# A fused recurrent-attention and cosine-gated MLP kernel: moving loads between queues and chunks

## The chip, the cores and the metric

The kernel runs on one core of a Trainium2 chip. The core has a matrix engine (TensorE, "PE" in the profile, with weight loads as "PEld"), three elementwise engines (VectorE or "DVE", ScalarE or "ACT", GpSimd or "POOL") and SyncE ("SP"), which in this kernel only issues transfers. Transfers can be issued from SP, ACT and GpSimd; in the profile the issuing is shown as SPq, ACTq and POOLq, and the transfer itself as DMA. The metric is the device time in microseconds of one launch.

## The reference

A linear recurrence over 768 steps for 4 x 8 heads of 40 channels, then a two-layer MLP whose activation is h cos(h).

```python
for t in range(S):
    y[:, :, t] = np.einsum('bhd,bhde->bhe', rt, state)
    Sa = np.einsum('bhde,bhe->bhd', state, at)
    state_decay = state * wt[:, :, None, :] - np.einsum('bhd,bhe->bhde', Sa, bt)
    state = state_decay + np.einsum('bhd,bhe->bhde', vt, kt)
...
h = x @ w_in          # x: the y of all heads, 3072 x 320; w_in: 320 x 2048
g = h * np.cos(h)
return g @ w_out      # 2048 x 320
```

The six inputs r, k, v, w (the decay), a and b have the form (4, 8, 768, 40) in float32; the two weight matrices are float64, and the kernel decodes the 64-bit words into float32 itself.

## The kernel before

**Tiling.** The sequence is cut into 24 chunks of 32 steps (C = 32, NCH = 24). In a chunk the recurrence becomes matrix products and the inverse of a triangular 32 x 32 matrix for each head. Four chunks share one inversion (a "quarter" q below is such a group of four chunks; there are six). The stages of a chunk are: p1 (w, a and b transposed, the matrix to be inverted), p2 (v, r and k, and the gram matrices), and main (t, q, x, s, z: the state transposed, read, solved and updated). The MLP is cut into pieces (first_a, first_b, second) that are put between the segments of the recurrence to keep TensorE filled.

**Order.** Everything is written out by hand: each engine runs its own instructions in program order. The function `step(work)` runs one segment and then counts down a list of postponed actions; `later(n, action)` puts an action at the end of the n-th step after it. Most transfers are issued in this way, so that n decides where in SP's queue they stand. A transfer that has to wait (for a buffer to be read, for data to be written) holds up all that SP has behind it.

**Inputs.** `load(c, names)` (lines 146 to 152) issues, for each named input of chunk c, four transfers of 40 KB, one for each batch. w, a and b have two buffers each in turn (nat_w0, nat_w1 and so on); chunks 2 and 3 use free space in the weight buffers w_in_sb and w_out_sb instead. So in the profile "w_out_sb<-in_b_dram" is b of chunks 2 and 3. For the first four chunks w is loaded as it is and its running products are made by a scan. From chunk 4 on the decays come already multiplied up: `ws_fetch(q)` (line 159) loads the decays of a quarter, 640 KB, into the single buffer ws; `ws_scan(q)` (line 166) multiplies them up on DVE; `ws_store(q)` (line 178) writes ws to a buffer wd in DRAM; and load reads w of chunks 4 and on from wd (the tile "wd" has two buffers). `scanned(q)` (line 906) calls the scan and postpones the store and the next fetch. Quarter 1 is scanned in the startup (line 996), quarter 2 in chunk 3 (line 1064).

**Weights.** `rounded` (line 224) decodes a block of 512 columns in four parts: fetch (the 64-bit words, line 237, up to 512 KB), taken (DVE splits off mantissa and exponent, lines 245 and 246; ACT makes exponent and sign), mantissa (DVE line 255, ACT line 258) and product (DVE line 261, GpSimd line 264). There are 20 blocks. Their parts are strung on a list, `w_steps`, in which product n is followed by the fetch of block n + 3 (from block 7 on), the mantissa of n + 1 and the taking of n + 2. From block 10 on the words rotate through three buffers (nt, u, inv), so the buffer of block n + 3 is free once the mantissa step of block n has read its words. The list is worked off a few parts at a time, in the startup and in chunks 1 to 3.

**Around the change.** The startup issues its loads in lines 182 to 201; GpSimd fills constants up to line 218. The loop over chunks begins at line 1049; for chunk 2 the segments are

```python
segs, fill = [t, F2, v, q, S2, k, M, x, M, F3, g, M, s, S3, M, z, M, M], (0, 2)
```

where M is an MLP piece. The MLP's input goes through DRAM: `tokens` (line 771) writes a chunk's output to xd (line 775) and `back` (lines 785 and 787) reads it as xT. TensorE's calls named busy, spare and "po<-idle" are filler matmuls on zeros.

Of the kernel before, what the change touches and what calls it, by code (L numbers as in the profile page):

```python
# [20 lines left out]
def kernel(  # L21
# [43 lines left out]
    nc = tc.nc  # L65
# [54 lines left out]
    for n, fill in (("w", 1.0), ("a", 0.0), ("b", 0.0)):  # L120
        for i in range(4):
            x = slice((i - 2) * H * DP, (i - 1) * H * DP)
            if i < 2:
                t = const.tile([P, H, DP], F32, tag=f"nat_{n}{i}", name=f"nat_{n}{i}")
            else:
                t = {
                    "w": w_in_sb[:, 0, late:], "a": w_in_sb[:, 1, late:], "b": late_out
                }[n][:, x].rearrange("p (h d) -> p h d", h=H)
# [4 lines left out]
    for n in "kvr":  # L133
        t = const.tile([P, H, D], F32, tag=f"nat_{n}", name=f"nat_{n}")
# [11 lines left out]
    def load(c, names, via=nc.sync, parts=range(B)):  # L146
        for n in names:
            for i in parts:
                at_c = src[n][i, :, c * C : (c + 1) * C, :]
                if n == "w" and c >= 4:  # L150
                    at_c = wd[c // 4][i, :, c % 4]
                via.dma_start(nat[n, c][blk[i], :, :D], at_c.rearrange("h t d -> t h d"))  # L152
# [3 lines left out]
    ws = const.tile([P, C, D], F32, tag="ws", name="ws")  # L156
    wd = {}

    def ws_fetch(q, via=nc.sync):
        n = 4 * C * D  # L160
        via.dma_start(
            ws.rearrange("p t d -> p (t d)"),
            bass.AP(w.tensor, w.offset + q * n, [[S * D, B * H], [C * D, 4], [1, C * D]]),
        )

    def ws_scan(q):
        n = 1
        while n < C:
            to = ws[:, 2 * n - 1 :: 2 * n]
            nc.vector.tensor_tensor(to, to, ws[:, n - 1 :: 2 * n], ALU.mult)  # L170
            n *= 2
        n = C // 4
        while n:
            to = ws[:, 3 * n - 1 :: 2 * n]
            nc.vector.tensor_tensor(to, to, ws[:, 2 * n - 1 : C - 1 : 2 * n], ALU.mult)
            n //= 2

    def ws_store(q):
        wd[q] = dram.tile([B, H, 4, C, D], F32, tag="wd", name="wd")
        nc.sync.dma_start(wd[q].rearrange("b h c t d -> (b h c) (t d)"), ws.rearrange("p t d -> p (t d)"))  # L180

    for c in range(2):
        load(c, "w", parts=range(2))
# [2 lines left out]
    load(1, "a", nc.scalar)  # L186
    for n, c in (("w", 2), ("w", 3), ("a", 2), ("a", 3), ("b", 2)):
        load(c, n)
    ws_fetch(1)
    load(3, "b")  # L190


# [24 lines left out]
    idle = const.tile([P, P], BF16, tag="idle", name="idle")  # L217
    nc.gpsimd.memset(idle, 0.0)
    tick = const.tile([P, 1], BF16, tag="tick", name="tick")

    WID = 512
    first_done, second_done = [], []
# [120 lines left out]
    def later(steps, work):  # L343
        waiting.append([steps, work])

    def step(work, of_inv=0, of_w=0, small=False):


        before = list(waiting)
        work()  # L350
        G["small"] = small and G["kind"]
        for w in before:
            w[0] -= 1
            if w[0] == 0:
                waiting.remove(w)
                w[1]()
        for steps, n in ((inv_steps, of_inv), (w_steps, of_w)):
            for _ in range(min(n, len(steps))):
                steps.pop(0)()
# [224 lines left out]
    def p2_in(c):  # L584
        for dst, m in ((vp, "v"), (rp, "r")):
            nc.gpsimd.tensor_copy(  # L586
                dst.rearrange("p (i f) d -> p f i d", f=2)[:, :, :, :D],
                nat[m, c].rearrange("p (f i) d -> p f i d", f=2),
            )
        landed(c)  # L590
# [312 lines left out]

        return [first_w, both_a, lambda: p1_b(c), lambda: p1_n(c)]

    def scanned(q):

        ws_scan(q)
        later(2, lambda: ws_store(q))
        if q + 1 < NCH // 4:  # L910
            later(12, lambda: ws_fetch(q + 1))

    def p2(c):
        def last():
# [14 lines left out]
    with tc.manual_schedule():  # L929
# [63 lines left out]
        w_work[1][0]()  # L993
        for seg in (other[1], *first[2:], *other[2:]):
            step(seg)
        scanned(1)
        p2_in(0)
        p2_kn(0)
        inv_space()
# [25 lines left out]
        busy(6)  # L1025
        step(z0, 0, 2)
        busy(4)
        for n, c, name in ((1, 4, "a"), (3, 4, "w"), (5, 5, "w"), (6, 5, "a"), (7, 5, "b"), (9, 4, "b")):
            later(n, lambda c=c, name=name: load(c, name))

        done = 0

# [8 lines left out]
        def allowed(c):  # L1041
            return done < len(pieces) and 2 * pieces[done][0] + 2 <= c
# [6 lines left out]
        for c in range(NCH):  # L1049
            t, q, x, s, z = main(c)  # L1050
            v, k, g = p2(c + 1) if c + 1 < NCH else [lambda: None] * 3
            q0 = c - c % 4 + 4
            fill, pn, pn4 = (1, 4), None, None
            if c == 0:
                segs = []
            elif c == 1:
                segs, fill = [t, F1, v, q, k, S1, x, g, s, z], (1, 4)
            elif c == 2:
                segs, fill = [t, F2, v, q, S2, k, M, x, M, F3, g, M, s, S3, M, z, M, M], (0, 2)
            elif c == 3:  # L1060
                pw4, pa4, pb4, pn4 = p1(4)
                pw, pa, pb, pn = p1(6)
                segs = [
                    t, pw4, M, q, pa4, M, x, lambda: scanned(2), M, s, pw, M, pb4, pa, M, pn4, M, z, M,
                    pb, v, pn, k, M, g,
                ]
                fill = (2, 3)
            elif c == 4:
                pw, pa, *p8 = p1(8)
                firsts = [lambda n=n: pair_first(4, n) for n in range(4)]  # L1070
                seconds = [lambda n=n: pair_second(4, n) for n in range(4)]
                F4, F5, F6, F7 = firsts
                S4, S5, S6, S7 = seconds
                segs = [
                    t, v, M, q, M, k, x, M, F4, M, S4, F5, M, s, F6, M, pw, F7, M, z, M, g, M, pa, S5, lambda: scanned(3),
                ]
                fill = (2, 0)
            elif c == 5:
                pw, pa = p1(10)[:2]
                pb, pn = p8  # L1080
                segs = [t, M, pb, q, M, pn, k, M, x, M, s, S6, M, z, M, S7, M, pw, v, M, g, pa, M]
            elif c % 4 == 0 and q0 < NCH:
                pb, pn = p1(q0)[2:]
                segs = [t, v, M, q, M, k, x, M, g, M, s, pb, M, z, M, pn, M, M]
                if q0 + 4 < NCH:
                    segs.insert(-1, lambda: scanned(c // 4 + 2))
            elif c % 4 == 1 and q0 < NCH:
                pw, pa = p1(q0 + 2)[:2]
                segs = [t, M, pw, q, M, x, k, M, s, v, M, z, M, pa, M, g, M, M]
            elif c % 4 == 2 and q0 < NCH:  # L1090
                pb, pn = p1(q0 + 2)[2:]
                segs = [t, M, pb, q, M, pn, v, M, x, M, s, k, M, g, M, z, M, M]
            elif c % 4 == 3 and q0 + 4 < NCH:
                pw, pa = p1(q0 + 4)[:2]
                segs = [t, M, pw, q, M, x, k, M, s, v, M, z, M, pa, M, g, M, M]
            else:
                segs = [t, v, M, q, M, x, k, M, g, M, s, M, M, z, M, M]
            n = len(segs)

            goal = 8 * (c + 1) - (18 if c < 19 else 20)  # L1100
            empty, places = 0, segs.count(M)
            if c > 3:
                empty = max(0, min(places - (goal - done), 2 if c < 8 else places))
                goal = max(goal, done + places - empty)
            place = 0
            if c == 19:
                shifted(N_PAD[c])
            for i, seg in enumerate(segs):
                kept_busy(FILL.get((c, i), 0))
                while seg is s and ("rt", c) not in G:  # L1110
                    if allowed(c):
                        piece(4, 0)
                    else:
                        inv_steps.pop(0)()
                while seg is pn4 and w_steps:
                    w_steps.pop(0)()
                if seg is not M:
                    G["kind"] = "q" if seg is q and c > 3 else "other"
                    step(seg, *((0, 0) if c < 3 and seg in (*firsts, *seconds) else fill), small=seg in (q, x, g, s, z, pn, pn4, *firsts, *seconds))
                    if seg not in (*firsts, *seconds) and (c < 2 or c == 2 and not done):  # L1120
                        busy({s: 6, q: 5, v: 4, k: 4, z: 4}.get(seg, 3))
                else:
                    place += 1
                    if place * empty // places > (place - 1) * empty // places:
                        continue
                    if allowed(c) and (c != 4 or done < 23):
                        piece(*fill)
                while i == n - 1 and c > 3 and done < goal and c != 4 and allowed(c):
                    piece(*fill)
                if seg is pn and (c == 3 or c > 4 and c % 4 == 2):  # L1130
                    inv_steps.extend(by_blocks(q0) if c == 3 else inverse(q0))
# [36 lines left out]
```

## Time and profile before

| what | value |
|---|---|
| median of 3 runs | 806.88 us (803.46 to 807.32) |
| the profiled execution | 806.77 us, of which the span of the profile is 805.0 us |
| PE busy | 752.7 us, 94% |
| DVE busy | 487.0 us, 60% |
| ACT busy | 387.8 us, 48% |
| POOL busy | 201.1 us, 25% |
| DMA | 55.78 MB, mean 69 GB/s |
| busy share of PE in 20 us slices, first to seventh, in tenths | 5 7 7 7 6 9 8, then 9 (the highest digit) but for the last |
| granted clock of TensorE | mean 0.973 |

Times in the views are microseconds from the span's start, with the duration behind them. In the chain of waits ("the chain of work that ended last") each line is what the work after it waited for; "issue" is time for which the profile shows no cause. In the timelines, a bracket at the end of a line gives the idle time of the engine before it and what ended it. In the table by stretches each row gives the stretch, its length, the busy time and the number of instructions of PE, PEld, DVE, ACT and POOL, the granted clock, the DMA share and GB/s.

### The profile page before, as it was taken

The numbers are of one execution on the slowest core, as the hardware profiler recorded it, in microseconds if no ns is written. First come the engines' busy times: TensorE is split into PE (matmuls) and PEld (weight loads), VectorE is DVE, ScalarE is ACT, GpSimd is POOL, SyncE is SP. The second block draws the span as 40 slices with busy tenths as digits, with TensorE's granted clock in tenths as the row PEclk, the third lists the DMA queues.
The fourth block names the chain that finished last, engine by engine and source line by source line (L and its number), as shares of the span: only waits on it lengthen the run. The fifth ranks groups of instructions, "written<-read, shape, count | busy, mean of one in ns | idle before, by whom it ended". The sixth has DMA issues, their size and how long they took to land.

```text
span 805.0 us, 39600 instructions
## 1 busy us (share of the span) xinstructions
PE 752.7 (94%) x17812; PEld 575.5 (71%) x17812; DVE 487.0 (60%) x1025; ACT 387.8 (48%) x723; POOL 201.1 (25%) x354
## 2 busy tenths in 40 slices
PE   5777698999999999999999999999999999999997
PEld 4544376777777777777777777777787777777775
DVE  8779658864734796553895644994346873333231
ACT  1337467555425435545435635535645445354352
POOL 5316535320322220330330230332131122201000
PEclk9688799999999999999999999999999999999999
DMA  8666552354253324334214314223220222101000
GB/s 114 176 162 149 143 145 74 57 121 65 59 125 58 66 38 71 72 92 67 60 40 69 94 36 72 53 45 69 46 46 21 46 46 49 24 17 34 19 17 16
DMA packets 183303, 55.78 MB, mean 69 GB/s; under 512 B 157152, under 2 KB 178656, under 8 KB 183136
## 3 DMA queue, kind: packets, MB, share of 16 engines
q1 hardware_dynamic: 177440, 52.11, 30.1%
q8 instruction: 140, 2.29, 1.2%
q10 hardware_dynamic: 5440, 0.82, 0.7%
q0 software_dynamic: 256, 0.33, 0.2%
q14 instruction: 27, 0.22, 0.1%
HBM read 42.07 MB, written 11.14 MB: 66 GB/s over the span
## 4 chain that ended last, share of the span: by engine, by line
PE 66%; DVE 18%; ACT 4%; issue 4%; DMA 3%; SPq 3%; POOL 1%; DVEq 0%; ACTq 0%; POOLq 0%
PE ph L101 23%; PE po L101 19%; PE x0ps L101 3%; PE dps L101 3%; SPq L152 3%; DVE inv_tmp L494 3%; DVE rw L395 3%; PE vT L330 3%; PE gram L101 2%; DVE inv L498 2%; PE sps L101 2%; PE nps L101 2%; PE qps L101 2%; PE sT L654 1%; DMA nat_a<-in_a_dram 1%
## 5 line engine op out<-in xcount | busy, mean ns | idle before, releaser
L101 PE MATMUL po<-w_out_sb,gT 128*128 128x320 f32 x768 | 223.1, 439 | 0.0
L101 PE MATMUL ph<-xT,w_in_sb 128*128 128x256 f32 x768 | 187.0, 388 | 0.3 <-issue 0.3
L101 PEld LDWEIGHTS po<-w_out_sb,gT 128*128 128x128 f32 x768 | 140.2, 190 | 54.2 <-issue 1.7
L101 PEld LDWEIGHTS ph<-xT,w_in_sb 128*128 128x128 f32 x768 | 140.1, 191 | 30.4 <-issue 12.5
L829 ACT ACTIVATE turns<-ph,rnd 128x512 f32<-128x512 f32 x96 | 64.1, 686 | 157.7 <-PE ph L101 157.3
L831 DVE SCALAR_TENSOR_TENSOR turns<-turns,ph 128x512 f32<-128x512 f32 x96 | 64.1, 685 | 111.7 <-ACT turns L829 111.4
L839 DVE TENSOR_TENSOR gT<-ph,turns 128x512 f32<-128x512 f32 x96 | 65.8, 687 | 39.1 <-ACT turns L836 39.1
L755 POOL TENSOR_TENSOR qz<-qz,wc 128x160 f32<-128x160 f32 x92 | 42.4, 480 | 167.1 <-DVE qz L754 166.5
L836 ACT ACTIVATE turns<-turns,half_pi 128x512 f32<-128x512 f32 x96 | 69.4, 723 | 3.1
L835 ACT ACTIVATE turns<-turns 128x512 f32<-128x512 f32 x96 | 60.2, 627 | 18.9 <-DVE turns L831 18.9
L101 PE MATMUL ph<-xT,w_in_tail 64*128 64x256 f32 (+1 forms) x512 | 54.9, 393 | 1.3 <-issue 1.3
L498 DVE TENSOR_TENSOR inv<-inv,inv_tmp 128x31 f32<-128x31 f32 (+15 forms) x124 | 51.2, 413 | 4.3
L754 DVE TENSOR_TENSOR qz<-dps,qz 128x160 f32<-128x160 f32 x92 | 29.2, 318 | 36.2 <-PE dps L101 36.0
L586 POOL COPY vp<-nat_v 128x320 f32<-128x320 f32 x24 | 11.9, 494 | 156.3 <-DMA nat_v<-in_v_dram 135.8
L494 DVE TENSOR_TENSOR inv_tmp<-u,inv 128x31 f32<-128x31 f32 (+15 forms) x124 | 48.6, 392 | 2.3
L395 DVE RECIPROCAL rw<-nat_w 128x320 f32<-128x320 f32 x20 | 42.9, 2144 | 0.1
L658 ACT COPY s<-sT 128x512 f32<-128x512 f32 x46 | 24.5, 585 | 35.1 <-PE sT L654 35.1
L101 PEld LDWEIGHTS ph<-xT,w_in_tail 64*128 64x128 f32 (+1 forms) x512 | 32.5, 160 | 10.4 <-issue 6.8
L766 POOL TENSOR_TENSOR yt<-yt,wb 128x512 f32<-128x512 f32 x24 | 31.9, 1329 | 22.3 <-DVE yt L761 22.3
L718 DVE TENSOR_TENSOR sm<-sps,su 128x128 f32<-128x128 f32 x48 | 11.7, 286 | 32.1 <-ACT sm L713 29.3
L396 POOL TENSOR_TENSOR bn<-nat_b,rw 128x320 f32<-128x320 f32 x22 | 20.1, 914 | 43.6 <-DVE rw L395 37.2
L642 ACT COPY vvm<-gram 128x256 f32<-128x256 f32 x24 | 8.8, 369 | 43.6 <-DVE ag L637 43.2
(136 smaller groups left out, 1127.9 us busy)
## 6 DMA issues: line engine op xcount, KB each, us to landing
words<-in_moe_w_in_dram SPq DMA_DIRECT2D x8, 512.0 KB
xd<-yt SPq DMA_DIRECT2D x48, 80.0 KB
out_dram<-ot SPq DMA_DIRECT2D x24, 160.0 KB
nat_k<-in_k_dram SPq DMA_DIRECT2D x92, 40.0 KB
nat_v<-in_v_dram SPq DMA_DIRECT2D x92, 40.0 KB
nat_r<-in_r_dram SPq DMA_DIRECT2D x92, 40.0 KB
nat_a<-in_a_dram SPq DMA_DIRECT2D x84, 40.0 KB
ws<-in_w_dram SPq DMA_DIRECT2D x5, 640.0 KB
```

Of the source, the lines that this page charges most:

```text
L101: nc.tensor.matmul(o, lhsT=lhsT, rhs=rhs, start=start, stop=stop, skip_group_check=True)
L395: nc.vector.reciprocal(rw, wn)
L494: nc.vector.tensor_tensor(tmp, u[:, j : j + 1, :j].to_broadcast([P, C - j, j]), x[:, j:, j : j + 1].to_broadcast([P, C - j, j]), ALU.mult,)
L498: nc.vector.tensor_tensor(x[:, j:, :j], x[:, j:, :j], tmp, ALU.subtract)
L754: nc.vector.tensor_tensor(z, pick(dp, 0, (2 * N72 + C, 2), (N72, 2), (1, D)), z, ALU.add)
L755: nc.gpsimd.tensor_tensor(z, z, wc.rearrange("p (f m b) -> p f m b", f=2, m=2)[:, :, :, bb] .unsqueeze(3).to_broadcast([P, 2, 2, D]), ALU. ...
L766: nc.gpsimd.tensor_tensor(yt.rearrange("p j b t -> p (j b) t"), yt.rearrange("p j b t -> p (j b) t"), wx, ALU.mult)
L829: nc.scalar.activation(n, u, ACTF.Identity, bias=rnd, scale=1.0)
L831: nc.vector.scalar_tensor_tensor(n, n, -ROUND, u, ALU.add, ALU.subtract)
L835: nc.scalar.activation(n, n, ACTF.Abs)
L836: nc.scalar.activation(n, n, ACTF.Sin, bias=half_pi, scale=-2.0 * math.pi)
L839: nc.vector.tensor_tensor(gT[:, 2 * e : 2 * e + 2].rearrange("p f t -> p (f t)"), us[e], ns[e], ALU.mult)
```

## The change

The fetch of decays for quarters 1 and 2 and the store of quarter 1 are issued by GpSimd instead of SP. The fetch for quarter 1 moves from between b of chunk 2 and b of chunk 3, on SP, to behind GpSimd's last constant; b of chunk 3 thus follows b of chunk 2 directly. The store of quarter 1 is postponed by 12 steps instead of 2, and the fetch of quarter 2 by 26 instead of 12. The loads of a, b and w for chunks 4 and 5 are registered at the start of chunk 2 instead of the end of the startup, with other numbers of steps and in another order. Quarter 2's store and the later fetches and stores stay on SP with their steps.

```diff
-    def ws_fetch(q, via=nc.sync):
+    def ws_fetch(q):
         n = 4 * C * D
-        via.dma_start(
+        (nc.gpsimd if q < 3 else nc.sync).dma_start(
             ws.rearrange("p t d -> p (t d)"),
...
     def ws_store(q):
         wd[q] = dram.tile([B, H, 4, C, D], F32, tag="wd", name="wd")
-        nc.sync.dma_start(wd[q].rearrange("b h c t d -> (b h c) (t d)"), ws.rearrange("p t d -> p (t d)"))
+        (nc.gpsimd if q == 1 else nc.sync).dma_start(wd[q].rearrange("b h c t d -> (b h c) (t d)"), ws.rearrange("p t d -> p (t d)"))
...
         load(c, n)
-    ws_fetch(1)
     load(3, "b")
...
     tick = const.tile([P, 1], BF16, tag="tick", name="tick")
+    ws_fetch(1)
...
-    def scanned(q):
+    def scanned(q, store=2, fetch=12):
 
         ws_scan(q)
-        later(2, lambda: ws_store(q))
+        later(store, lambda: ws_store(q))
         if q + 1 < NCH // 4:
-            later(12, lambda: ws_fetch(q + 1))
+            later(fetch, lambda: ws_fetch(q + 1))
...
-        scanned(1)
+        scanned(1, 12, 26)
...
-        for n, c, name in ((1, 4, "a"), (3, 4, "w"), (5, 5, "w"), (6, 5, "a"), (7, 5, "b"), (9, 4, "b")):
-            later(n, lambda c=c, name=name: load(c, name))
...
             elif c == 2:
+                for n, m, name in ((2, 4, "w"), (3, 4, "a"), (5, 5, "w"), (7, 5, "a"), (9, 4, "b"), (11, 5, "b")):
+                    later(n, lambda m=m, name=name: load(m, name))
```

## Prediction

> **What bounds the kernel now.** I read the page, then the chain of waits in order of time, then the timelines of SP, DVE, GpSimd and TensorE for the first 170 us, then the DMA busy share by tens of microseconds. From about 133 us TensorE is busy 92 to 100% of every stretch and its filler matmuls are fixed instructions, so what is won or lost earlier shifts everything behind it by the same amount. The change moves transfers only (the program's TensorE and DVE instructions stay the same 2621 and 932 rows in both listings), so it can pay only where somebody waits for a transfer, before 133 us. Two such places carry the argument. First the chain at the start, then the same chain around 90 us:
>
> ```profile
> 21.32 3.65 DMA w_out_sb<-in_b_dram
> 25.13 0.96 POOL bn L396
> 26.14 1.13 PE bT L330 x4
> 30.93 1.04 ACT nt L459 x2
> 31.99 1.26 DVE u L486
> ...
> 86.40 5.80 DMA words<-in_moe_w_in_dram
> ...
> 93.06 0.61 DVE w_out_sb L261
> ...
> 93.74 0.63 POOL w_out_sb L264
> ...
> 96.35 1.89 PE sT L654 x6
> ```
>
> At the start, the last piece of b of chunk 3 (it lands in w_out_sb) needs 3.65 us and releases GpSimd's product, the transposes, and DVE's u. At 86.40 a word block of w_in takes 5.80 us and releases the decoding of weights. What SP did before that issue, and what DVE and TensorE did meanwhile:
>
> ```profile
> 18.99 0.68 SPq L161 DMA_DIRECT2D ws<-in_w_dram  x1
> ...
> 79.06 3.28 SPq L152 DMA_DIRECT2D nat_a<-in_a_dram  x4
> 82.38 1.93 SPq L152 DMA_DIRECT2D nat_r<-in_r_dram  x4
> 84.41 1.89 SPq L152 DMA_DIRECT2D nat_b<-in_b_dram  x4
> 86.40 0.39 SPq L237 DMA_DIRECT2D words<-in_moe_w_in_dram  x1
> ```
> ```profile
> 78.35 0.68 DVE L255 SCALAR_TENSOR_TENSOR mant<-words,mant 128x512 f32<-128x512 uint32 x1
> ...
> 86.20 0.87 DVE L255 SCALAR_TENSOR_TENSOR mant<-words,mant 128x512 f32<-128x512 uint32 x1
> 92.30 0.43 DVE L245 TENSOR_SCALAR mant<-words 128x512 int32<-128x512 int32 x1 [5.22 <-DMA words<-in_moe_w_in_dram]
> ```
> ```profile
> 92.48 0.38 PE L101 MATMUL busy<-idle 128*128 128x512 bf16 x1 [3.64 <-issue]
> ...
> 95.37 0.69 PE L654 MATMUL sT<-ident,qz 128*128 128x128 f32 x2 [2.02 <-DVE yt L761]
> ```
>
> The block fetched at 86.40 is the eleventh (number 10); its buffer (nt) was freed by the mantissa step of block 7, at 78.35 + 0.68 = 79.03. SP was not waiting for a buffer but issuing loads of chunks 3 to 5 without a pause from 73.8 to 86.3. DVE stood still for 5.22 us, and its additions to the state (L754), queued behind, with it.
>
> **What the Trainium skill says.** "Runtime: NRT & Kernel Launch", Instruction fetch mechanics: instructions come in blocks of 16 KiB, 256 instructions, over a DMA queue of the sequencer, mostly hidden. The trace agrees on the block (the instruction queue q8: 140 packets, 2.29 MB, 16.4 KB each) but not on hidden: TensorE's "issue" waits inside runs of equal matmuls are 0.9 to 2.1 us at 50.8, 56.9, 64.0, 72.4 and 76.4, and 3.64 at 88.8, each ending 2.2 to 3 us after such a packet. "DMA: Bandwidth & Descriptors", Queues, rings and completion order: each DMA engine takes turns between queues by packet. So an instruction block stands behind data in flight; the longest wait falls where two word blocks and eight nat loads are in flight. "SBUF — State Buffer", SBUF: two separate sides: descriptors of a DMA issued from GpSimd are written by GpSimd, and some DVE operations lock it out. The trace of before has only eight such issues, 4.78 us in all, 0.60 each, and no such clash.
>
> **The change part by part.**
>
> *Fetch of ws for quarter 1, from SP to GpSimd.* SP loses 0.68 us ahead of b of chunk 3, and 640 KB that filled the 16 engines from about 20.9 to 23 (74 and then 100% busy, by the DMA view). b of chunk 2, with nothing such in front, landed some 1.7 us after its last issue; b of chunk 3 took 3.65. With the last issue at 20.6 it lands near 22.5 instead of 24.97. Then what is late next: the reciprocal at L395 ends at 23.02, and TensorE reaches this transpose at 24.5 (bT of chunk 2 begins at 23.85). The transpose moves from 26.14 to 24.5, DVE's u from 31.99 to about 30.4; the ws scan ends at 29.28 and is no obstacle. Gross gain 1.6. Against it: the 640 KB now run around 11.5 to 13.5 us, where the engines are 77% busy with chunks 1 to 3, and 1.7 us of them must go between. The slack there is 0.5 us for w (ACT's copies end at 15.3, DVE takes them at 15.9) and 1.3 for a (wn ends at 19.6, its reciprocal starts at 20.87). I take a loss of 0.4, net 1.2, ends 0.2 and 1.9. On GpSimd the issue stands before copies that are needed at 12.66 (aT): 1.8 us of slack against 0.6 for an issue.
>
> *Store of quarter 1, from SP at 34.73 to GpSimd behind rp of 62.81.* Behind it stand kn (L593), the copy at L594 and weight products; kn ends at 64.73 and its transpose starts at 68.23, so 0.6 us is hidden, even 2 us would be. On SP 1.34 us leave a stretch that DVE's inversion bounds: 0. Its transfer now lies beside DVE-bound work (58 to 87 us): 0.
>
> *Fetch of quarter 2, from SP at 55.16 to GpSimd behind the product of 102.99.* It frees 1.55 us of SP and 640 KB around the TensorE waits at 50.8 and 56.9: 0.2, ends 0 and 1.3. GpSimd is idle 2.5 us after its new place. The scan that needs it starts at 149.60: 46 us of cover.
>
> *The six loads of chunks 4 and 5 (24 issues of 0.47 us, 11.3 us of SP at least) leave 56 to 88 us.* Behind block 9, SP keeps only v and r of chunk 3 (8 x 0.48, done by 77.6), so block 10 is issued at 79.1 and lands by 85 even at 5.80 us. DVE needs it at 86.20 + 0.87 = 87.07 instead of 92.30: 5.2 us. Late next: GpSimd's state products would start at 89.7 instead of 94.86, so sT could run at 91.2; but TensorE has its own wait at 88.84. The block it waits for is asked for about 87.0; in the new order blocks 11 and 12 are in flight then, without nat loads. I take 1.8 of the 3.64 us, so TensorE is back at 90.6, has 1.0 of filler, and runs sT at 91.7: gain 4.6. Ends: 3.0 (the wait stays) and 5.2.
>
> *The same loads in chunk 2.* In the listing for SP, w and a of chunk 4 now stand between the store of xd and the return xT, which feeds the first ph matmuls. Eight issues are 3.8 us; SP idled 1.6 of them at 99.9 to 101.5 waiting for xd. So xT is issued 2.2 us later against the rest; it was issued by 103.0, lands about 2 us later, and is needed at 106.94, so 1.9 of cover: 0.3, ends 0 and 1.5 (the ws fetch meets it). Blocks 14 to 17 stand behind further loads. By SP's sum they land at 106.6, 115.5, 119.5 and 122, against needs (shifted by 4.6) of 106.7, 114.8, 118.4 and 125.9. DVE then waits 0.7 and 1.1, in front of idle gaps of 1.16 and 1.12 us: 0.2, up to 1.5. Last, TensorE's instruction blocks. Here it is never idle between 97 and 123, with packets of q8 every 4 to 5.5 us; DMA is 44 and 67% busy:
>
> ```profile
> 100.00:110.00 10.00, 10.00 (x315) 7.50 (x310) 5.67 (x9) 7.23 (x13) 5.44 (x5) 0.99 0.44 111
> 110.00:120.00 10.00, 10.00 (x296) 8.40 (x287) 6.14 (x13) 6.47 (x12) 1.42 (x2) 1.00 0.67 186
> ```
>
> The last number but one is the DMA share. A nat load of 40 KB costs some 3.4 us of one engine (141 to 161 us: 30% of 16 engines for 28 loads), so 24 of them and the ws fetch add about 110 of the 16 x 25 us: 80% or more. [...] I take 0.8 us over the five blocks, ends 0 and 5 x 1.5 = 7.5. Loss of the part: 0.3 + 0.2 + 0.8 = 1.3.
>
> *Sum.* -1.2 - 0.2 - 4.6 + 1.3 = -4.7 us. The profiled execution took 806.77 (span 805.0 and 1.8 around it), the median is 806.88, 0.1 above: 802.
>
> **The rivals.** (A) *The gap closes only to TensorE's own wait, and chunk 2 asks for more.* For it: 3.64 us of "issue" lie in the same gap. Against: most waits of that kind are under 2.1. Start -0.8, gap -3.0, chunk 2 +1.9: 805. (B) *All of it pays.* For it: DVE and ACT have idle gaps of 1 to 3 us all through chunk 2, and the waits at 50.8 to 57.8 shrink too. -1.9 - 1.0 - 5.2 + 0.3 = -7.8: 799. (C) *Slower: instruction blocks in chunk 2.* One mechanism: loads put into the one stretch in which TensorE has no slack delay its instruction fetches, five by 1.5 us (7.5) and the one in dps by 3.6, as at 88.84, 11 in all, against 6.0 won before: 812. It decides as soon as these waits exceed 6 us. For it: the DMA share; against: no such wait in 106 to 120, with word blocks at 74 to 82% in pieces of it. (D) *The loads of chunks 4 and 5 come late for chunk 3*: w is transposed at 133.32, a at 140.70, and both land by 115: excluded but for a percent.
>
> **How the numbers follow.** The forecast has 0.45, A 0.25, B 0.15, C 0.15. Noise of this kernel is about 0.5%, 4 us; the three runs shown span 3.9. Faster by more (below 802.9): most of B and two thirds or more of the forecast's and some of A's spread, 0.55. Within: 0.31. Slower by more: 0.14, C. The range 797.5 to 807.5 holds the forecast, A and B, and leaves most of C out.
>
> **What would show it.** Right: the 5.22 us of DVE gone; block 10 issued near 78 on SP; sT about 91 minus 1.2; DVE's u near 30.5; from there to the end the same distances. Wrong: TensorE "issue" waits of 1 us and more between 95 and 125, ph waiting for xT, or DVE for blocks 15 and 16, by more than 1.3 together; or a startup in which DVE is no longer dense from 10 to 23 us.

## The result, and the profile after

The change made the kernel slower. The median of 12 runs is 812.37 us (808.32 to 814.95), of before in the same session 805.55 (801.89 to 811.40); the ratio is 1.0079, 95% interval 1.0054 to 1.0104. The profiled span grew from 805.0 to 810.3 us. 802 with a range to 807.5 was predicted, so the sign was wrong.

The lines that answer to those of before, first from the chain of waits (start, duration, what the work after it waited for):

```profile
6.79 3.92 DMA w_in_sb<-in_w_dram
...
34.06 1.26 DVE u L486
...
123.39 4.85 DMA words<-in_moe_w_in_dram
128.34 0.43 DVE mant L245
...
129.95 2.19 PE dps L101 x108
...
133.36 6.10 PE po L101 x16
139.46 0.87 PE sT L654 x8
```

DVE's u starts 2.1 us later than before, not 1.6 earlier, and behind w of chunk 3. The word block that the chain now waits for is not the one at 86 us but one at 123, in chunk 2. The timeline of TensorE shows the two places:

```profile
16.73 0.78 PE L330 MATMUL wT<-ident,w_in_sb 128*128 128x128 f32 x4 [2.85 <-DMA w_in_sb<-in_w_dram]
...
127.79 0.45 PE L101 MATMUL dps<-idle 32*64 32x288 bf16 x4 [3.86 <-DVE sm L718]
129.95 0.45 PE L101 MATMUL dps<-idle 32*64 32x288 bf16 x4 [1.71 <-DVE rt L567]
...
133.29 6.17 PE L101 MATMUL po<-w_out_sb,gT 128*128 128x320 f32 x16
```

The same places before, without a wait, and with shorter po matmuls behind them:

```profile
12.90 2.07 PE L330 MATMUL wT<-ident,w_in_sb 128*128 128x128 f32 x8
...
124.93 0.33 PE L101 MATMUL dps<-idle 32*64 32x288 bf16 x8
...
128.04 4.57 PE L101 MATMUL po<-w_out_sb,gT 128*128 128x320 f32 x16
```

The timeline of DVE after the change, first around the gap of before, then in chunk 2:

```profile
89.57 0.87 DVE L255 SCALAR_TENSOR_TENSOR mant<-words,mant 128x512 f32<-128x512 uint32 x1
90.36 0.67 DVE L245 TENSOR_SCALAR mant<-words 128x512 int32<-128x512 int32 x1
...
111.88 0.43 DVE L245 TENSOR_SCALAR mant<-words 128x512 int32<-128x512 int32 x1 [2.34 <-DMA words<-in_moe_w_out_dram]
...
124.02 0.43 DVE L245 TENSOR_SCALAR mant<-words 128x512 int32<-128x512 int32 x1 [3.92 <-DMA words<-in_moe_w_out_dram]
...
128.34 0.43 DVE L245 TENSOR_SCALAR mant<-words 128x512 int32<-128x512 int32 x1 [0.70 <-DMA words<-in_moe_w_in_dram]
```

The first two lines are the mantissa step of block 9 and the taking of block 10: the wait of 5.22 us between them is gone, as forecast. The other three are the taking of blocks 14, 15 and 16: 6.96 us for which DVE stood still. Before, the same three waited for nothing:

```profile
111.30 0.42 DVE L245 TENSOR_SCALAR mant<-words 128x512 int32<-128x512 int32 x1
...
119.43 0.42 DVE L245 TENSOR_SCALAR mant<-words 128x512 int32<-128x512 int32 x1
...
122.95 0.52 DVE L245 TENSOR_SCALAR mant<-words 128x512 int32<-128x512 int32 x1
```

What stood in SP's queue there, after:

```profile
104.39 2.26 SPq L152 DMA_DIRECT2D nat_k<-in_k_dram  x4
106.77 2.11 SPq L237 DMA_DIRECT2D words<-in_moe_w_out_dram  x3
108.92 1.91 SPq L152 DMA_DIRECT2D nat_w<-wd  x4
110.93 3.23 SPq L152 DMA_DIRECT2D nat_v<-in_v_dram  x4
114.20 2.85 SPq L152 DMA_DIRECT2D nat_r<-in_r_dram  x4
117.16 1.87 SPq L152 DMA_DIRECT2D nat_a<-in_a_dram  x4
119.14 2.20 SPq L237 DMA_DIRECT2D words<-in_moe_w_out_dram  x2
121.43 1.86 SPq L152 DMA_DIRECT2D nat_b<-in_b_dram  x4
123.39 0.39 SPq L237 DMA_DIRECT2D words<-in_moe_w_in_dram  x1
```

And before, where the same word blocks have fewer loads in front of them:

```profile
103.11 2.98 SPq L152 DMA_DIRECT2D nat_k<-in_k_dram  x4
106.19 1.34 SPq L237 DMA_DIRECT2D words<-in_moe_w_out_dram  x3
107.64 2.82 SPq L152 DMA_DIRECT2D nat_v<-in_v_dram  x4
110.50 1.94 SPq L152 DMA_DIRECT2D nat_r<-in_r_dram  x4
112.54 1.72 SPq L237 DMA_DIRECT2D words<-in_moe_w_out_dram  x2
114.37 1.95 SPq L237 DMA_DIRECT2D words<-in_moe_w_in_dram  x2
```

After, SP issues from 96.96 to 126 without a pause, and the chain of waits runs through these issues from 99.71 to 123.39: SP is the bound of this stretch. Landmarks on TensorE, by the start of a stage in both profiles, tell where the time went:

| stage | before | after | after - before |
|---|---|---|---|
| sps of chunk 1 | 80.23 | 83.75 | +3.5 |
| qps of chunk 2 | 102.71 | 99.63 | -3.1 |
| qps of chunk 3 | 137.64 | 143.94 | +6.3 |
| last sT (chunk 23) | 729.44 | 735.26 | +5.8 |

So: 3.5 us lost up to chunk 1, 6.6 won over the gap, 9.4 lost in chunk 2, and about nothing after. The 9.4 is the firm one of these: the stretch from qps of chunk 2 to qps of chunk 3 took 34.9, 35.1 and 35.0 us in the three profiles that have the loads where before has them. The 3.5 is not: in the seven profiles without the early fetch, sps of chunk 1 starts anywhere from 77.78 to 82.75.

### The profile page after: what moved, and what is told of

It is laid out like the page before. It is cut to its first block, busy times and chain, and to the rows that moved or that the text cites. A ratio compares the mean times of both kernels' runs of the same rounds, so it can differ in the third digit from the quotient of the medians.

```text
span 810.3 us, 39602 instructions
## 1 busy us (share of the span) xinstructions
PE 754.1 (93%) x17812; PEld 577.0 (71%) x17812; DVE 488.5 (60%) x1025; ACT 386.9 (48%) x723; POOL 200.6 (25%) x357
## 3 DMA queue, kind: packets, MB, share of 16 engines
q8 instruction: 140, 2.29, 1.2%
q0 software_dynamic: 688, 2.29, 1.0%
## 4 chain that ended last, share of the span: by engine, by line
PE 68%; DVE 14%; issue 4%; ACT 4%; DMA 4%; SPq 3%; POOL 2%; DVEq 0%; ACTq 0%; POOLq 0%
PE ph L101 23%; PE po L101 21%; PE x0ps L101 4%; PE dps L101 3%; PE gram L101 3%; DVE rw L395 2%; SPq L152 2%; PE vT L330 2%; DVE inv_tmp L494 2%; PE sps L101 2%; DVE inv L498 2%; PE nps L101 2%; PE qps L101 2%; PE sT L654 1%; PE kT L330 1%
## 5 line engine op out<-in xcount | busy, mean ns | idle before, releaser
L831 DVE SCALAR_TENSOR_TENSOR turns<-turns,ph 128x512 f32<-128x512 f32 x96 | 64.0, 684 | 112.1 <-ACT turns L829 111.8
L754 DVE TENSOR_TENSOR qz<-dps,qz 128x160 f32<-128x160 f32 x92 | 29.1, 316 | 35.2 <-PE dps L101 35.1
L658 ACT COPY s<-sT 128x512 f32<-128x512 f32 x46 | 24.5, 584 | 35.1 <-PE sT L654 35.1
L101 PEld LDWEIGHTS <-idle 128*128 128x128 bf16 (+2 forms) x268 | 17.7, 98 | 20.4 <-issue 14.4
L718 DVE TENSOR_TENSOR sm<-sps,su 128x128 f32<-128x128 f32 x48 | 11.7, 285 | 32.8 <-ACT sm L713 30.0
```

The costliest lines, as they stand in the source:

```text
L101: nc.tensor.matmul(o, lhsT=lhsT, rhs=rhs, start=start, stop=stop, skip_group_check=True)
L754: nc.vector.tensor_tensor(z, pick(dp, 0, (2 * N72 + C, 2), (N72, 2), (1, D)), z, ALU.add)
L831: nc.vector.scalar_tensor_tensor(n, n, -ROUND, u, ALU.add, ALU.subtract)
```

## The experiments

All ratios are to the kernel before on the same chip, 5 rounds unless said otherwise.

**e1: the early fetch alone**

```diff
-    ws_fetch(1)
     load(3, "b")
...
     tick = const.tile([P, 1], BF16, tag="tick", name="tick")
+    ws_fetch(1, nc.gpsimd)
```

> The kernel before with one part of the change: the fetch of quarter 1 is issued by GpSimd behind its last constant, and b of chunk 3 follows b of chunk 2 on SP. Theory: the 640 KB run ahead of w of chunk 3, TensorE waits about 2.9 us for it at 13.9 us, DVE's u starts at 34.1 instead of 32.0, and the 2.4 us stay to the end: ratio 1.003 (1.001 to 1.005). Rival (the startup's loss is taken up by the later wait for word block 10, where SP is the bound): u late all the same, but sT of chunk 1 at 95.4 and ratio 1.000.

Ratio 1.0020 (0.9994 to 1.0045). The timeline of TensorE:

```profile
12.91 1.06 PE L330 MATMUL wT<-ident,w_in_sb 128*128 128x128 f32 x4
16.19 1.09 PE L330 MATMUL wT<-ident,w_in_sb 128*128 128x128 f32 x4 [2.22 <-DMA w_in_sb<-in_w_dram]
```

The wait for w of chunk 3 is there, but u starts at 32.29, 0.3 later than before, not 2.1. Part of the delay is thus taken up inside the startup, and what lasts is not separated from zero by this run. So u at 34.1, as the theory had it, was not found, and its 2.4 us that stay are neither shown nor excluded.

**e2: the six loads alone**

```diff
-        for n, c, name in ((1, 4, "a"), (3, 4, "w"), (5, 5, "w"), (6, 5, "a"), (7, 5, "b"), (9, 4, "b")):
-            later(n, lambda c=c, name=name: load(c, name))
...
             elif c == 2:
+                for n, m, name in ((2, 4, "w"), (3, 4, "a"), (5, 5, "w"), (7, 5, "a"), (9, 4, "b"), (11, 5, "b")):
+                    later(n, lambda m=m, name=name: load(m, name))
```

> The kernel before with one part of the change: the six loads of chunks 4 and 5 in chunk 2, everything of ws as before. Theory: the 5.2 us wait of DVE for word block 10 goes, and blocks 14 to 16, behind the loads in SP's queue, come 7 us late in chunk 2: -5.9 and +9.4, ratio 1.004 (1.002 to 1.007). Rival (chunk 2's loss comes from GpSimd's transfer of quarter 2, which lies there too): the gap goes and nothing is given back, ratio 0.994.

Ratio 1.0048 (1.0027 to 1.0068). The waits of DVE between 97 and 140 us (total, times, longest):

```profile
DVE mant L245 <- DMA words<-in_moe_w_out_dram: 5.7, 2, 3.9
```

No wait for block 10, and qps of chunk 2 at 95.64 instead of 102.71; then 43.4 us to qps of chunk 3, where before took 34.9. This part carries both signs by itself, without any transfer of GpSimd's in chunk 2: the rival falls as the cause of this loss.

**e4: the fetch of quarter 1 on SP, behind b of chunk 3**

```diff
-        (nc.gpsimd if q < 3 else nc.sync).dma_start(
+        (nc.gpsimd if q == 2 else nc.sync).dma_start(
...
     load(3, "b")
+    ws_fetch(1)
...
-    ws_fetch(1)
```

> The changed kernel with the fetch of quarter 1 back on SP, but behind b of chunk 3 instead of ahead of it. Theory: w of chunk 3 lands in time, and b of chunk 3 lands near 22.5, so u starts near 30.4 and 4 us of the changed kernel's startup go: ratio to before 1.003 (1.000 to 1.005). Rival (the startup waits for b, or the fetch is not what delays it): ratio stays at 1.008.

Ratio 1.0056 (1.0038 to 1.0073). TensorE no longer waits for w of chunk 3, and u starts at 31.30. The 30.4 of the theory is not reached: DVE now waits 2.3 us for ws itself (the scan stands in front of u), and TensorE 2.5 us for no visible cause in nps. The waits of 6.4 and 0.9 us for words in chunk 2 stay. Of 4 us expected, 0.0023 of 805 us = 1.9 came, with intervals that overlap.

**e5: as e4, the loads further back in chunk 2**

```diff
-                for n, m, name in ((2, 4, "w"), (3, 4, "a"), (5, 5, "w"), (7, 5, "a"), (9, 4, "b"), (11, 5, "b")):
+                for n, m, name in ((12, 4, "w"), (13, 5, "w"), (15, 4, "a"), (16, 5, "a"), (17, 4, "b"), (18, 5, "b")):
```

> As the one with the fetch behind b, and the six loads of chunks 4 and 5 moved further back in chunk 2 (steps 12, 13, 15, 16, 17, 18), where SP's queue has them behind word block 16 and between the last blocks. Theory (place in SP's queue): blocks 14 to 16 come as early as before, nothing is given back in chunk 2, ratio 0.991 (0.988 to 0.995), about 799 us. Rival (load on the DMA engines: the same bytes in the same 30 us): TensorE and DVE still wait in chunk 2, ratio near that of the fetch behind b, 1.003.

Ratio 0.9982 (0.9957 to 1.0008), 0.0074 or 6.0 us better than e4. The stretch from qps of chunk 2 to qps of chunk 3 fell from 43.0 to 37.1 us, and DVE's waits for words there from 7.3 to 2.2. The direction is the theory's; the size of 0.991 was not reached. Blocks 15 and 16 waited for nothing, but 2.2 us for block 14 stayed, although none of the moved loads stands in front of it on SP any more (next section).

**e6: the kernel before, with the six loads at steps 12 to 18 of chunk 2 as in e5, and nothing else**

> The kernel before with one edit: the six loads of chunks 4 and 5 at steps 12 to 18 of chunk 2; the fetches and stores of ws all as before. Theory (place in SP's queue decides): DVE's wait for word block 10 goes, blocks 14 to 16 are not delayed, the startup is that of before: ratio 0.995 (0.992 to 0.998). Rival (the earlier time of GpSimd's fetch and store, or b ahead of the fetch, was what helped in e5): no better than 0.999.

Ratio 0.9955 (0.9935 to 0.9974), median 801.85 us over 22 runs: faster than both kernels. No wait for words is left anywhere between 56 and 140 us. SP's timeline shows why (from word block 15 on):

```profile
107.97 0.87 SPq L237 DMA_DIRECT2D words<-in_moe_w_out_dram  x2
108.95 0.37 SPq L237 DMA_DIRECT2D words<-in_moe_w_in_dram  x1
109.42 2.78 SPq L152 DMA_DIRECT2D nat_w<-wd  x4
112.31 0.38 SPq L237 DMA_DIRECT2D words<-in_moe_w_in_dram  x1
```

Blocks 15 and 16 go out back to back, and the first moved load comes behind them, where SP otherwise waits for word buffers. The 6.7 us gained by qps of chunk 3 (130.92 instead of 137.64; 1.4 of them were there at u already) shrink to 4.7 by wT at 239 us and 3.7 in the span; where the rest goes was not followed up.

**e7: as e4, the six loads issued by GpSimd at the changed kernel's steps**

```diff
-                    later(n, lambda m=m, name=name: load(m, name))
+                    later(n, lambda m=m, name=name: load(m, name, nc.gpsimd))
```

> As e4_fetch_behind_b, with the six loads at the changed kernel's steps 2 to 11 of chunk 2, but issued by GpSimd instead of SP: the same bytes from the same place in the program, none of SP's time. Theory (SP's issuing is what delays blocks 14 to 16): DVE's waits for words in chunk 2 fall from 7.3 us to under 2.5, TensorE's wait of 4 us at dps goes, ratio 1.001 or lower, if GpSimd's own 14 us of issuing do not hold up its weight products. Rival (the load on the DMA engines): waits and ratio stay, 1.0056.

Ratio 0.9986 (0.9969 to 1.0002), 0.0070 or 5.6 us better than e4. The table by stretches of e7 (length, busy and count of PE, PEld, DVE, ACT, POOL, clock, DMA share, GB/s):

```profile
110.00:120.00 10.00, 8.87 (x273) 7.40 (x271) 6.23 (x12) 7.94 (x16) 8.31 (x15) 1.00 1.04 214
120.00:130.00 10.00, 6.00 (x146) 4.14 (x146) 6.52 (x19) 5.91 (x11) 4.71 (x9) 0.75 0.64 144
```

The DMA engines are full (1.04) between 110 and 120, against 0.53 in e4, and still DVE's waits for words fell to 1.2 us: what delayed the words in the changed kernel was their place behind SP's issuing, not the load on the DMA engines. But e7 is not free of cost: from qps of chunk 2 to qps of chunk 3 it took 40.3 us, 5.4 more than before. In it TensorE waited 1.6 us for rt and 2.4 for "issue" at dps (1.27 before, at the same place), and the clock fell. Whether the full DMA engines or GpSimd's issuing made those waits longer was not separated.

**e8: the changed kernel with the six loads at steps 12 to 18**

> The changed kernel with the six loads at steps 12 to 18 of chunk 2 and nothing else. Beside e5_loads_late (0.9982) it differs only in the fetch of quarter 1, which GpSimd issues early. Theory: w of chunk 3 waits some 2.5 us behind the 640 KB and the run loses 1 to 2.5 us on e5: ratio 1.0005 (0.999 to 1.002). Rival (the early fetch costs nothing that lasts): 0.998.

Ratio 0.9991 (0.9965 to 1.0017). The wait for w of chunk 3 is 3.1 us, u starts at 33.24. Against e5 the early fetch costs 0.0009, 0.7 us, which the intervals do not separate from nothing. So the theory's 1 to 2.5 us are neither shown nor excluded. But the one edit repairs the changed kernel: 1.0079 becomes 0.9991, 7 us. Blocks 15 and 16 waited for nothing; for block 14 DVE waited 2.7 us.

**e9: the kernel before, profiled again** (a single run)

> The kernel before, profiled once more, to see how far the waits that the prediction was read from hold: DVE's wait for word block 10 was 5.2 us in one profile, and 3.7 us in the profile of e1_fetch_only, which has the same loads. If it is 3 to 4 us here, the gain was over-read by 1 to 2 us; if it is 5 us or more, it was not.

DVE waited 3.1 us for block 10 and 1.2 for block 11. Block 10 alone thus cost 5.2, 3.7 (e1) and 3.1 us in three profiles with these loads, both blocks together 5.2, 4.5 and 4.2: the 5.2 us of the prediction was the upper end, by 1 to 2 us.

**All runs beside each other.** The stretches (us) are those of the two signs: from sps of chunk 1 to qps of chunk 2, with the gap, and from there to qps of chunk 3. The waits are DVE's for blocks 12 to 16.

| run | the six loads | gap stretch | chunk 2 stretch | waits for words | ratio |
|---|---|---|---|---|---|
| before | as before | 22.5 | 34.9 | 0 | 1 |
| e9 | as before | 22.8 | 35.0 | 0 | |
| e1 | as before | 21.0 | 35.1 | 0.3 | 1.0020 |
| e6 | SP, steps 12 to 18 | 18.6 | 34.6 | 0 | 0.9955 |
| e5 | SP, steps 12 to 18 | 16.1 | 37.1 | 2.2 | 0.9982 |
| e8 | SP, steps 12 to 18 | 16.4 | 39.3 | 2.7 | 0.9991 |
| e7 | GpSimd, steps 2 to 11 | 15.5 | 40.3 | 1.2 | 0.9986 |
| e4 | SP, steps 2 to 11 | 16.6 | 43.0 | 7.3 | 1.0056 |
| e2 | SP, steps 2 to 11 | 16.3 | 43.4 | 5.7 | 1.0048 |
| after | SP, steps 2 to 11 | 15.9 | 44.3 | 7.0 | 1.0079 |

Every kernel without the loads ahead of block 10 has the gain in the first stretch; the three that have them on SP at steps 2 to 11 lose 8.1 to 9.4 us in the second, and only these are slower than before by more than their intervals.

## Why the prediction was wrong, point by point

**The gap at 86 us: right.** Block 10 was issued at 82.48, with a startup 2.1 us later, and the wait of DVE went in every kernel with the loads moved. 4.6 us were forecast; the stretch from sps of chunk 1 to qps of chunk 2 shrank by 6.6 (after), 6.2 (e2) and 3.9 (e6), from 22.5 in before. As e1 and e9 show, the 5.22 us that this was read from were 1 to 2 us above other profiles of the same loads. TensorE's own wait in that gap, 1.8 in the forecast, was 1.7 in place of 3.64.

**The loads in chunk 2: the step that failed**, in the term "By SP's sum they land at 106.6, 115.5, 119.5 and 122 ... DVE then waits 0.7 and 1.1, in front of idle gaps". The mechanism, its place and the blocks were named; the term was priced at 0.2, at most 1.5, and the part at 1.3. The part measured 8.4 us in e2 and 9.4 in after. Measured from sT of chunk 2 (91.7 in the forecast, 94.63 in the trace), blocks 15 and 16 were to land after 23.8 and 27.8 us; DVE could take them after 29.4 and 33.7. The first error was the price of an issue on SP. I had put 0.48 us for one, 1.92 for a group of four. The nine groups between 97 and 126 us took 20.6 us, 2.29 each, with single issues of 1.4 to 1.7 us in the chain (1.61 at 110.93, 1.37 at 114.69, 1.72 at 119.14), and the three issues of block 14 took 2.11 in place of 1.4. Every group in front of a block adds its excess, and seven stood in front of block 15: 16.9 us in place of 13.4. With the blocks' own issues, 2.11 in place of 1.4 and 2.20 in place of about 1.0, that is 5.4 of the 5.6 us by which block 15 was later than forecast. Its last issue ended at 121.33 and DVE took it 2.7 us later; the forecast's sum, done again, leaves 2.9 for that. So the transfer was priced rightly, the issuing was not. The profile of before had such groups too (2.98 for nat_k at 103.11, 2.82 for nat_v at 107.64); I took the shortest ones for the price. The prediction's own view has one more, 3.28 for nat_a at 79.06.

The second error in that step was the cover. The idle gaps of 1.16 and 1.12 us behind the waits are themselves waits for ACT (at sm, L718, and at turns, L831). They stand in after with the same 1.16 and 1.12 us: they moved along and hid nothing. sm (L718), rt (L567) and with them dps stood behind the late blocks, and TensorE waited 3.86 + 1.71 = 5.6 us. Then its clock was lower (last section): the 16 po matmuls behind took 6.17 us in place of 4.57. Those 5.6 and 1.6 make 7.2 of the 9.4 us; 1.6 more are the waits of ph at 105 and 117 (1.0 and 0.6). The first is the wait for xT, which SP issues behind w and a of chunk 4; e2's profile names it there, with 1.55 us. That term stood at 0.3, up to 1.5. The third term, 0.8 us for TensorE's instruction blocks, did not come (see the rivals).

**The startup: wrong in sign.** The forecast had the 640 KB squeezed in for "a loss of 0.4", by a slack of 0.5 us. All three profiles with the early fetch (after, e1, e8) have TensorE waiting 2.85, 2.22 and 3.1 us for w of chunk 3; none of the other seven do. Between 10 and 20 us the DMA share rose from 0.77 to 0.92, and SP, which waits for earlier transfers before it issues more, waited 5.1 us for w in place of 2.1. That fits what the Trainium skill states in "DMA: Bandwidth & Descriptors", Queues, rings and completion order, that an engine takes turns between queues by packet: here a queue with rows of 5 KB would take its turns against one with rows of 160 B. The wait is shown by the three profiles; this cause of it was not tried by itself. The gain on the other side was overrated as well: with b in front of the fetch (e4, e5, e7), u started at 31.30, 32.26 and 32.09, not at 30.4, and DVE then waited 2.1 to 2.3 us for ws. With before's order u started at 30.62 (e6) to 31.99, so b's place gained nothing that can be seen. With the early fetch it started at 32.29 (e1), 33.24 (e8) and 34.06 (after). What the early fetch costs in the end is small: 0.0020 (e1), 0.0009 (e8 against e5) and 0.0023 (after against e4), on average 1.4 us, and no single pair settles it.

**Store of quarter 1 and fetch of quarter 2 on GpSimd: open.** The forecast had 0 for the store and a gain of 0.2 for the fetch. e4 has both and e2 has neither, at 1.0056 and 1.0048, but there block 14 is late behind the loads in any case. Where the loads are out of its way, in e5 and e8, GpSimd's fetch stands just ahead of it, and it is late again; in e6, without that fetch, it is not. First e5, then e6:

```profile
101.09 2.67 SPq L237 DMA_DIRECT2D words<-in_moe_w_out_dram  x3
...
108.18 0.43 DVE L245 TENSOR_SCALAR mant<-words 128x512 int32<-128x512 int32 x1 [2.16 <-DMA words<-in_moe_w_out_dram]
```
```profile
100.03 2.84 SPq L237 DMA_DIRECT2D words<-in_moe_w_out_dram  x3
...
105.20 0.43 DVE L245 TENSOR_SCALAR mant<-words 128x512 int32<-128x512 int32 x1 [0.17 <-DVE x L696]
```

SP's issues of block 14 ended 12.0 us (e5), 10.5 (e8) and 11.8 (e6) after sT of chunk 2, so SP is not what differs. GpSimd issued the 640 KB at 100.53 in e5 and at 100.75 in e8, 0.6 and 1.0 us ahead of the block. The ratios, 0.9982 and 0.9991 against 0.9955, point the same way, but the intervals overlap and these kernels differ in the startup too; no run moves this fetch alone. The three issues on GpSimd took 0.58 to 0.61 us in the changed kernel, the 0.60 of the forecast; of the lock-out that the skill's page "SBUF — State Buffer", SBUF: two separate sides, describes, no line there shows a trace.

**The rivals.** C forecast 812 and 812.37 was measured, but not by its mechanism: TensorE's "issue" waits between 97 and 133 us were 1.1 in all, against 1.6 before. The right number came from a wrong cause. D was excluded, rightly: no stage of chunk 3 waited for the loads by more than 0.7 us.

**The parts together.** e2 gives +3.9 us (0.0048), the fetch about +1.4, the sum 5.3; measured 6.4 (0.0079), which the intervals allow. The premise that all won or lost before 133 us lasts to the end held in after (6.3 us at qps of chunk 3, 5.8 at the last sT), but less well in other profiles: e6 kept 3.7 of 6.7 us, and e7, 1.0 behind before at qps of chunk 3, has a span 2.4 us shorter.

## What to carry to other kernels

When transfers are moved out of one crowded stretch of a queue, add up the queue in the stretch they go to, group by group, with the mean price of an issue there and not the shortest one, and look at which transfer in it has a consumer with no slack. Order in an issuing queue can matter more than the load on the DMA engines: with the same bytes 6 to 15 us later (e6) the words waited for nothing, and from another queue (e7), with the DMA engines full, 1.2 us in place of 7.3. That is not a free place, though: e7's chunk 2 was still 5.4 us longer than before. Idle gaps of an engine behind a delayed operation are cover only where what ends them does not depend on that engine.

## What the runs showed of the hardware that was not expected

TensorE's granted clock falls after a few us of waiting, as the Trainium skill tells in "TensorE: Matmul & The Clock Gate", Part 1: the clock is halved by a monitor when the engine has been idle and returns after some us of work. What was not expected is that waits of 3.9 and 1.7 us in an otherwise dense stretch are enough. The table by stretches of after, with these waits before 130, and the same stretches before:

```profile
120.00:130.00 10.00, 4.42 (x124) 3.17 (x120) 4.12 (x11) 3.16 (x7) 2.41 (x4) 0.82 0.79 209
130.00:140.00 10.00, 9.29 (x155) 6.88 (x155) 8.45 (x18) 6.21 (x11) 5.14 (x7) 0.67 0.35 108
```
```profile
120.00:130.00 10.00, 8.39 (x284) 6.28 (x276) 7.14 (x21) 7.94 (x14) 4.83 (x8) 1.00 0.33 95
130.00:140.00 10.00, 9.52 (x131) 8.15 (x129) 9.91 (x15) 6.50 (x11) 5.26 (x5) 1.00 0.19 60
```

The clock (last number but two) is 0.82 and 0.67 after, and 1.00 in both before and in e6; e2, e4 and e7 show 0.70 to 0.75 in the first stretch. The waits of 5.6 us so cost 1.6 us more than their length in the po matmuls alone.

A load of 40 KB takes SP 0.45 us to issue in the median, but about one in ten takes 1.0 us or more (52 of 548 before, 57 of 548 after, up to 2.2). What makes them long was not tried and stays open.
